# A build-time plan that holds a product back a little behind the silu step it reads: other orders on all engines of one core

## Chip, cores and metric

The kernel runs on 1 core of one Trainium2 chip. The metric is the device time of one execution in microseconds. Before the change it took 378.16 us, the median of 3 runs (378.05 to 378.83).

## What is computed

Causal attention with a forget gate, whose result goes straight into a SwiGLU block. The reference, cut to what matters:

```python
# q, k, v: (8, 8, 576, 64), f: (8, 8, 576)
cum = cumsum(log(clip(f, 1e-4, 1.0)), axis=-1)
scores = q @ k^T / sqrt(64) + cum[:, :, :, None] - cum[:, :, None, :]
attn = softmax(where(causal, -1e9, scores))
x = (attn @ v).transpose(0, 2, 1, 3).reshape(4608, 512)
g = x @ w_gate                                # 512 x 1536
out = (g * sigmoid(g) * (x @ w_val)) @ w_out  # 1536 x 512, float32
```

The inputs and the output are float32; the kernel's matrix products read bf16 and gather in float32.

## The kernel before

**Who sets the order.** The kernel is written as a list of steps, each made by `op` (L304) with the engine or engines that may run it and a cost in us for each (`act`, `dve`, `mm`, `pool`, around L313). A step names the steps that it reads (`after`), the buffers that it takes and those that it uses, and a `key`. When the kernel is built, `Plan.run` (L77) plays all steps through in a model of time: whenever an engine is free, it takes the ready step with the lowest key whose buffers can be had, and issues its instructions. The order of the instructions on each engine, and which PSUM bank or SBUF buffer a step gets, come out of this play. On the chip nothing of the modelled times is left; each engine runs its instructions in the order that it was given, and semaphores hold a reader until its data is there. A long table, `ORDER`, replaces the keys of single steps by their number; the change leaves it alone.

**When a reader becomes ready.** In the model a step ends at `busy[e]`, the time at which its engine is free for the next one. Its results are there `PIPE` later (0.2 for PE, 0.17 ACT, 0.12 DVE, 0.11 POOL), and readers on another engine, or on one of several, become ready only then. A reader whose single engine is the one that has just run the step becomes ready at `busy[e]` itself, that is, in time for the very next place on that engine. These two cases are the two pushes of the event "done":

```python
push(busy[e], "done", (o, e, True))
push(o.done, "done", (o, e, False))
```

**The work.** PE does all matrix products, ACT the exponentials and tanh, DVE (VectorE) the products of the SwiGLU, POOL (GpSimd) masks and some copies and sums, SP most of the DMAs.

- *Attention*, head by head: `score` (PE, L703) in four groups of 320 to 512 columns, `expo` (ACT, L737), `mask` of the diagonal blocks (POOL, L746), `weigh` (PE, L760), which sums the values by the weights into a bank of which there is one ("o"), `invert` and `scale` (DVE, L767 and L772), which read that bank and free it, and then a transpose into `xT`: on PE by `flip` (L777), or by a DMA on SP, `cross` (L790). The heads' queries and keys come over DMAs: `narrow` (POOL's queue, L590), `turned` (SP, L599), and `rows`, the rows of decay (SP, L602).
- *The SwiGLU*, in nine token tiles of 512 tokens and twelve column blocks each. `unit` makes one block: a gate product (four matmuls of 512 columns, PE, L918), `tanh` of half the gate (ACT, L922), the `silu` step on DVE (L932), th = (th + 1) * gate, a value product (PE, L918 again), and `times` (DVE, L935), hh = th * 0.5 * value. From block 6 of tile 6 on ACT does the whole silu (L925) and DVE has no silu step. Banks for gate and value products come from a pool of four ("f").
- *The output products*. Tiles 0 to 2 take w_out as it is (`project`, PE, L976, and copies on ACT). Tiles 3 to 8 (`finish`) make seven products of halves instead of eight: DVE first makes blends of the weights once (`blend`, L948) and three sums of each pair of hh (`sums`, L960); PE makes the products (L969), and the halves are put together by ACT (`mid_copy`, L985), POOL (`both` and `apart`, L992 and L1017) and DVE (`more` and `close`, L996 and L1020) and stored by SP (L1023).

Silu and `times` have the key -5, `sums` 50000 and `blend` 40000 and up; the plan so takes a sum or a blend on DVE only where no SwiGLU step is ready.

Of the kernel before, what the change touches and what calls it, by code (L numbers as in the profile page):

```python
# [34 lines left out]
class Plan:  # L35
# [9 lines left out]
    def op(self, eng, fn, after=(), behind=(), take=(), use=(), key=0.0, ready=0.0, dma=None):  # L45
        o = Op(eng, fn, list(after), behind, list(take), list(use), key, ready, dma)
        for b in o.use:
            b.left += 1
        self.ops.append(o)
        return o  # L50
# [26 lines left out]
    def run(self, idle=None):  # L77
# [9 lines left out]
        busy = {e: 0.0 for e in engines}  # L87
# [5 lines left out]
        left, t, seq = len(self.ops), 0.0, 0  # L93
        events = []

        def push(at, kind, o):
            nonlocal seq
            seq += 1
            heapq.heappush(events, (at, seq, kind, o))
# [9 lines left out]
        while left:  # L109
# [3 lines left out]
            t = events[0][0]  # L113
            while events and events[0][0] <= t + 1e-9:
                _, _, kind, o = heapq.heappop(events)
                if kind in ("queue", "dma"):
                    for r, share in shares():
                        r[0][0] -= (t - moved) * share
                        while r and r[0][0] < 1e-6:
                            over, n = r.pop(0)  # L120
# [27 lines left out]
                elif kind == "done":  # L148
                    o, e, own = o
# [6 lines left out]
            for e in engines:  # L156
                while busy[e] <= t + 1e-9:
                    k = kind_of.get(e)
                    full = k and lanes[k][taken[k] % 8] > t
                    if e == "SP" and full:  # L160
                        break
                    ready[e] = [o for o in ready[e] if o.start is None]
                    best = None
                    for o in sorted(ready[e], key=lambda o: (o.key, o.n)):
                        if o.dma is not None and full:
                            continue
                        if self._takes(o, t):
                            best = o
                            break
                    if best is None:  # L170
                        break
                    o = best
                    o.start, o.ran = t, e
                    dur = o.eng[e]
                    if e == "PE":
                        dur *= self.clock(t)
                        self._fill(idle, busy[e], t)
                    o.fn(e)
                    busy[e] = end = t + dur
                    for s in o.then:  # L180
                        s.wait -= 1
                        if not s.wait:
                            push(max(t, s.ready), "ready", s)
                    if o.dma is not None:
                        o.lane = taken[k] % 8
                        lanes[k][o.lane] = 1e9
                        taken[k] += 1
                        push(max(end + (0.53 if o.tag == "f" else 0.9), T_SW if e == "POOL" else 0.0), "queue", o)
                        push(busy[e], "wake", None)
                    else:  # L190
                        o.done = end + self.PIPE[e]
                        push(busy[e], "wake", None)
                        push(o.done, "end", o)
                        push(busy[e], "done", (o, e, True))
                        push(o.done, "done", (o, e, False))
        return max(o.done for o in self.ops)

# [24 lines left out]
def kernel(ctx, tc, q, k, v, f, w_gate, w_val, w_out, out):  # L222
# [78 lines left out]
        lambda t: 2.0 if t < TWARM else 1.0,  # L301
    )

    def op(eng, fn, *args, tag=None, packet=20.0, **kw):  # L304
        if not isinstance(eng, dict):
            eng = {eng[0]: eng[1]}
        o = plan.op(eng, lambda e: fn(e, *args), **kw)
        o.tag, o.packet = tag, packet
        return o

    E = {"ACT": nc.scalar, "DVE": nc.vector, "POOL": nc.gpsimd, "SP": nc.sync, "PE": nc.tensor}
# [1 line left out]
    def act(n):  # L313
        return 0.055 + n / 1200

    def dve(n, psum=True):
        return (n + (75 if psum else 58)) / 960

    def mm(*cols):
        return sum(c / 2400 + 0.0025 for c in cols)  # L320
# [98 lines left out]
    def gates(parts, key):  # L419


        lds = [op(("ACT" if n % 2 else "SP", 0.45), ld_f, n, key=-1e4 + n, dma=0.1, packet=100, tag="f") for n in range(4)]
        ld1 = op(("SP", 0.5), ld_f, None, key=-39, dma=LD1, packet=50, ready=LD1_AT, behind=lds[2:3], tag="f1")
        done, s, lns = [], None, []
        for i, c in enumerate(parts):
# [42 lines left out]
    def blank(e, what):  # L468
# [46 lines left out]
        else:  # L515
            if what != "rest":
                fill32(e, VB[what][:, :, :, D:].bitcast(F32), ONE2)
            if what:
# [4 lines left out]
              after=[op(("DVE", 0.07), lambda e: nc.vector.memset(warm, 1.0), key=-30)])  # L523
# [507 lines left out]
    def unit(t, fc, t0, n, hs, lo, kk, after):  # L1031
        if (t, fc) == ALONE:
            tabled.append(op(("ACT", 1.4), turn_table, after=before + exps, key=-6, tag="table"))
        needs = [o for a, b, done in x_ready.values() if a < t0 + n and b > t0 for o in done]
        wr = [w_ready["g", fc // FCG], w_ready["v", fc // FCG]]
        bg, bv, bt = Buf(*F_POOLS(t)), Buf(*F_POOLS(t)), Buf("th")
        p, r = divmod(fc, 2)
        fresh = hs[p] is None
        if fresh:
            hs[p] = Buf("hh")  # L1040
            hs[p].first = None
        g = op(("PE", mm(*[n] * KD)), gate, wg, fc, t0, n, bg, after=needs + wr + after, behind=[] if fresh else [hs[p].gate], take=[bg] + ([hs[p]] if fresh else []), key=kk, tag=("gp", t, fc))
        if fresh:
            hs[p].gate = g
        alone = (t, fc) >= ALONE
        if alone:
            b = op(("ACT", act(n)), whole, n, bg, bt, after=[g] + tabled, take=[bt], use=[bg], key=-5, tag=("tanh", t, fc))
        else:
            b = op(("ACT", act(n)), tanh, n, bg, bt, after=[g], take=[bt], use=[bg], key=-5, tag=("tanh", t, fc))
            before.append(b)  # L1050
            b = op(("DVE", dve(n)), silu, n, bg, bt, after=[b], use=[bg, bt], key=-5, tag=("silu", t, fc))
        a = op(("PE", mm(*[n] * KD)), gate, wv, fc, t0, n, bv, after=[g], take=[bv], key=kk + 1, tag=("vp", t, fc))
        m = op(("DVE", dve(n)), times, n, bv, bt, hs[p], r, lo, 1.0 if alone else 0.5, after=[a, b, hs[p].first],
               use=[bv, bt, hs[p]], key=-5, tag=("mul", t, fc))
        if fresh:
            hs[p].first = m
        read.append((t0, t0 + n, [g, a]))
        return g, m
# [3 lines left out]
    def ffn(t, t0, n):  # L1062
        key, hs, ms = 1e5 * (t + 1), [None] * (KF // 2), []
        for fc in range(KF):
            parts = [(0, HALF), (HALF, n - HALF)] if t == 0 and fc < WIDE else [(0, n)]
            ms.append([])
            for u, (lo, w) in enumerate(parts):
                lg, m = unit(t, fc, t0 + lo, w, hs, lo, key + 100 * fc + 50 * u, [last_gate[0]])
                ms[fc].append(m)
        last_gate[0] = lg  # L1070
        tails.append((t, t0, key, hs, ms))
# [3 lines left out]
    def simple(t, t0, key, hs, ms):  # L1075
        for q in range(2):
            bo = Buf("ot")
            for h in range(2):
                bf, a = Buf("f"), None
                for g in range(0, KF // 2, 2):  # L1080
                    a = op(("PE", mm(*[DM] * 4)), project, hs, q, h, bf, (g, g + 1),
                           after=[x for m in ms[2 * g : 2 * g + 4] for x in m] + [w_ready["o", c] for c in range(NCO)] + [a],
                           take=[] if g else [bf], use=[hs[g], hs[g + 1]] + ([bf] if g else []), key=key + 2000 + 200 * q + 100 * h + g, tag=("fo", t, q, h))
                plain.append(a)
                c = op(("ACT", act(DM)), out_copy, h, bf, bo, after=[a] + (o_out2 + regrouped if t == 0 else []), take=[] if h else [bo],
                       use=[bf] + ([bo] if h else []), key=-4, tag=("ot", t, q, h))
                op(("SP", 0.7), store, t0 + h * HALF + q * P, h, bo, after=[c], use=[bo], key=-4, dma=1.0, packet=90, tag=("out", t, q, h))
# [95 lines left out]
    for t, t0 in enumerate(range(0, N_TOK, MT)):  # L1183
        ffn(t, t0, MT)
    for r in tails[:QUICK]:
        simple(*r)
    ready = [w_ready["o", c] for c in range(NCO)]
    blended = [op({e: f((KF // 2) * HALF // 2) + 0.35 * (n // 2 == 1) for e, f in BLEND_ON.items()}, blend, n, after=ready, key=BLEND_KEY + n, ready=BLEND_AT, tag=("blend", n)) for n in range(6)]
    blended += [op({e: f((KF // 2) * HALF // 2) for e, f in BLEND_ON.items()}, blend, n, after=blended[:6] + plain, key=BLEND_KEY + n, ready=BLEND_AT, tag=("blend", n)) for n in range(6, 10)]
    for r in tails[QUICK:]:  # L1190
        finish(*r, blended)
# [17 lines left out]


QUICK = 3


def F_POOLS(t):
    return ("f",) + tuple((x, WIDE_AT, 1e9) for x in "sot")
# [152 lines left out]
```

## Time and profile before

| | before |
|---|---|
| median of 3 runs | 378.16 us |
| the profiled execution | 378.08 us |
| its span, from the first to the last instruction | 376.4 us |
| granted TensorE clock, mean | 1.00 |
| busy DVE, of the span | 249.4 us, 66% |
| `times` (L935): count, mean of one | 112, 667 ns |
| `silu` on DVE (L932): count, mean of one | 82, 656 ns |
| `sums` (L960): count, mean of one | 108, 384 ns |

The profile is one execution. A row in order of time gives the start from the span's begin and the length, both in us, then engine, line, operation, what is written and read, shapes, and how many of the same stand together; in brackets the time for which the engine waited ahead of it and what ended that wait. A line of stretches gives from:to and length, and then for PE, the weight loads of PE, DVE, ACT and POOL the busy time and the number of instructions, after that the granted clock, the mean share of the DMA engines, and GB/s. The chain of waits is the work that ended last, followed back from the end, each step to what released it. Ends of matmuls are modelled, and so is the busy time of PE.

### The profile page before, as it was taken

To read this page: it belongs to the slowest core of one execution; us is meant where nothing else is said; L and a number is where in the kernel's file an instruction comes from. 1 tells how busy PE (TensorE), PEld (TensorE's weight loads), DVE (VectorE), ACT (ScalarE), POOL (GpSimd) and SP (SyncE) were. 2 spreads that over 40 slices of the span, in tenths; PEclk is the share of its full clock that TensorE was granted. 3 is DMA by queue.
4 is the path that set the end of the run, shared out by engine and by line. 5 is a ranking of instruction groups with operands and counts; after the bars stand their busy time and mean duration, and the time that the engine had idled before them with its cause. 6 is when DMAs were issued, how large, how long until landed. Compare 5 with 4: busy or idle time off the path is not lost.

```text
span 376.4 us, 9092 instructions
## 1 busy us (share of the span) xinstructions
PE 368.8 (98%) x3427; PEld 233.6 (62%) x3427; DVE 249.4 (66%) x575; ACT 214.4 (57%) x438; POOL 161.4 (43%) x388
## 2 busy tenths in 40 slices
PE   8999999999999999999999999999999999999996
PEld 5667655455565555555685558655887776467465
DVE  7979886277526674499737994598638844753664
ACT  7999962265656754746576467555774433333332
POOL 8897546033633643465376437732462013003000
PEclk9999999999999999999999999999999999999999
DMA  8999998859988998999699999995325003002003
GB/s 145 192 198 195 206 204 151 185 100 180 174 187 169 166 189 160 228 191 180 117 160 200 228 149 143 243 206 99 72 74 93 2 2 111 2 0 81 33 0 114
DMA packets 125163, 52.01 MB, mean 138 GB/s; under 512 B 111823, under 2 KB 119695, under 8 KB 124351
## 3 DMA queue, kind: packets, MB, share of 16 engines
q1 hardware_dynamic: 108478, 35.95, 49.2%
q0 software_dynamic: 16288, 15.14, 26.9%
q8 instruction: 27, 0.44, 0.5%
q10 hardware_dynamic: 352, 0.34, 0.3%
q14 instruction: 18, 0.14, 0.1%
HBM read 38.56 MB, written 17.07 MB: 148 GB/s over the span
## 4 chain that ended last, share of the span: by engine, by line
PE 94%; DMA 2%; DVE 1%; POOL 1%; ACT 1%; issue 1%; DVEq 0%; POOLq 0%
PE ps L918 49%; PE ps L969 14%; PE ps L703 10%; PE ps L976 8%; PE ps L760 8%; DMA su<-in_k_dram 2%; PE ps L721 1%; PE ps L777 1%; PE ps L578 1%; POOL su L554 1%; PE ps L729 0%; PE ps L1201 0%; ACT PT L737 0%; DVE hh L935 0%; DVE xn L772 0%
## 5 line engine op out<-in xcount | busy, mean ns | idle before, releaser
L918 PE MATMUL ps<-xT,wv 128*128 128x512 bf16 (+2 forms) x496 | 111.7, 351 | 0.0
L918 PE MATMUL ps<-xT,wg 128*128 128x512 bf16 (+2 forms) x496 | 111.5, 351 | 0.0
L737 ACT ACTIVATE PT<-ps 128x384 bf16<-128x384 f32 (+2 forms) x192 | 91.6, 510 | 14.8 <-PE ps L703 9.7
L935 DVE SCALAR_TENSOR_TENSOR hh<-th,ps 128x512 bf16<-128x512 f32 (+1 forms) x112 | 74.5, 667 | 21.1 <-PE ps L918 12.9
L922 ACT ACTIVATE th<-ps 128x512 f32<-128x512 f32 (+1 forms) x82 | 47.2, 577 | 54.1 <-PE ps L918 51.8
L746 POOL TENSOR_SCALAR_AFFINE_SELECT PT<-PT 128x128 bf16<-128x128 bf16 (+1 forms) x192 | 54.1, 288 | 44.1 <-ACT PT L737 38.5
L918 PEld LDWEIGHTS <-wg 128*128 128x128 bf16 x496 | 45.1, 97 | 37.9
L918 PEld LDWEIGHTS <-wv 128*128 128x128 bf16 x496 | 45.0, 97 | 38.1
L932 DVE SCALAR_TENSOR_TENSOR th<-th,ps 128x512 f32<-128x512 f32 (+1 forms) x82 | 53.7, 656 | 19.7 <-ACT th L922 19.6
L703 PE MATMUL ps<-QK 68*128 68x256 bf16 x392 | 63.9, 261 | 0.4 <-ACT PTa L737 0.4
L746 POOL TENSOR_SCALAR_AFFINE_SELECT PTa<-PTa 128x256 bf16<-128x256 bf16 x64 | 26.3, 413 | 80.3 <-ACT PTa L737 79.5
L760 PE MATMUL ps<-VB,PT 128*128 128x65 bf16 x768 | 42.0, 193 | 0.0
L703 PEld LDWEIGHTS <-QK 68*128 68x128 bf16 x392 | 31.5, 97 | 14.0 <-issue 0.6
L760 PEld LDWEIGHTS <-PT 128*128 128x128 bf16 x768 | 34.2, 97 | 9.3 <-POOL PT L746 0.9
L737 ACT ACTIVATE PTa<-ps 128x384 bf16<-128x384 f32 x64 | 30.9, 488 | 15.4 <-PE ps L703 14.8
L767 DVE RECIPROCAL rc<-ps 128x5 f32<-128x5 f32 (+2 forms) x68 | 12.8, 188 | 39.6 <-PE ps L760 39.3
L969 PEld LDWEIGHTS <-su 128*128 128x128 bf16 x360 | 34.8, 97 | 4.6
L960 DVE TENSOR_TENSOR su<-hh 128x512 bf16<-128x512 bf16 (+1 forms) x108 | 36.7, 384 | 0.9
L925 ACT ACTIVATE th<-ps 128x512 f32<-128x512 f32 x30 | 17.9, 596 | 32.1 <-PE ps L918 32.1
L976 PE MATMUL ps<-wo,hh 128*128 128x512 bf16 x144 | 34.8, 379 | 0.0
L772 DVE TENSOR_TENSOR xn<-ps,rc 128x320 bf16<-128x320 f32 (+2 forms) x72 | 32.4, 454 | 2.2
L969 PE MATMUL ps<-wt,su 128*128 128x256 bf16 x216 | 29.0, 272 | 0.0
(97 smaller groups left out, 323.1 us busy)
## 6 DMA issues: line engine op xcount, KB each, us to landing
out_dram<-ot SPq DMA_DIRECT2D x32, 256.0 KB
natv<-in_v_dram SPq DMA_DIRECT2D x25, 256.0 KB
qk_d<-in_q_dram POOLq DMA_DIRECT2D x24, 144.0 KB, 3.6
qk_d<-in_k_dram POOLq DMA_DIRECT2D x24, 144.0 KB, 4.3
wv<-in_moe_w_val_dram POOLq DMA_DIRECT2D x3, 512.0 KB, 10.6
wg<-in_moe_w_gate_dram POOLq DMA_DIRECT2D x3, 512.0 KB, 12.4
wo<-in_moe_w_out_dram POOLq DMA_DIRECT2D x4, 384.0 KB, 14.1
VB<-in_v_dram POOLq DMA_DIRECT2D x7, 128.0 KB, 8.9
```

What stands on the lines that cost most here:

```text
L703: nc.tensor.matmul(s[:, c : c + w], QK[:KR, hqk[p].i, 1, j * S + kt * P : j * S + (kt + 1) * P], QK[:KR, hqk[p].i, 0, j * S + q0 : j * S + ...
L737: nc.scalar.activation(place(h, i)[:, OFFS[i] : OFFS[i] + c], ps(bs)[:, :c], AF.Exp, scale=0.125)
L746: nc.gpsimd.affine_select(out=d, in_=d, pattern=pat, compare_op=ALU.is_ge, fill=0.0, base=0, channel_multiplier=-1,)
L760: nc.tensor.matmul(o[:, lo : lo + D + 1], pt[:, c : c + P], VB[hvb[b].i][:, kt, hb, : D + 1], start=first and n == 0, stop=last and n == l ...
L772: nc.vector.tensor_mul(XN[bx.i][:, qb : qb + nq, j], o, r)
L918: nc.tensor.matmul(ps(bf)[:, a:b], w[:, ko, fc * P : (fc + 1) * P], xT[:, ko, at : at + b - a], start=ko == 0 and a == 0, stop=ko == KD - ...
L922: nc.scalar.activation(TH[bt.i][:, :n], ps(bf)[:, :n], AF.Tanh, scale=0.5)
L932: nc.vector.scalar_tensor_tensor(out=t, in0=t, scalar=1.0, in1=ps(bf)[:, :n], op0=ALU.add, op1=ALU.mult)
L935: nc.vector.scalar_tensor_tensor(out=HH[bh.i][:, r, lo : lo + n], in0=TH[bt.i][:, :n], scalar=by, in1=ps(bf)[:, :n], op0=ALU.mult, op1=ALU ...
L960: E[e].tensor_tensor(out=o, in0=x, in1=y, op=f)
L969: nc.tensor.matmul(ps(bf)[:, c * HALF : (c + 1) * HALF], left(g)[:, q * P : (q + 1) * P], right[:, g], start=opens and g == 0, stop=g == K ...
L976: nc.tensor.matmul(ps(bf), HH[hs[g].i][:, r, lo : lo + P], wo[:, 2 * g + r], start=g + r == 0, stop=2 * g + r == KF - 1)
```

## The change

The event that tells a reader on the same engine that its data is there is pushed `o.raw` later. Only one kind of step has a `raw` that isn't 0: `silu` on DVE, with the new constant RAW = 0.17. Its one reader on the same engine is the `times` of the same block. In the model the engine still is free at `busy[e]`, so a step that is ready then is taken, and `times` is ready 0.17 us later. Nothing else changes in the list of steps; the orders and buffers that the plan deals out are made anew. Lines after 1211 stand one lower.

```diff
-                        push(busy[e], "done", (o, e, True))
+                        push(busy[e] + o.raw, "done", (o, e, True))
                         push(o.done, "done", (o, e, False))
...
-    def op(eng, fn, *args, tag=None, packet=20.0, **kw):
+    def op(eng, fn, *args, tag=None, packet=20.0, raw=0.0, **kw):
...
-        o.tag, o.packet = tag, packet
+        o.tag, o.packet, o.raw = tag, packet, raw
...
-            b = op(("DVE", dve(n)), silu, n, bg, bt, after=[b], use=[bg, bt], key=-5, tag=("silu", t, fc))
+            b = op(("DVE", dve(n)), silu, n, bg, bt, after=[b], use=[bg, bt], key=-5, raw=RAW, tag=("silu", t, fc))
...
 QUICK = 3
+RAW = 0.17
```

## The prediction

> **What bounds the kernel now.** I read the page first: its list of engines, then the chain that ended last. After it the busy time of each engine by stage, and last the order in time around each place where PE stops.
>
> ```profile
> span 376.4 us, 9092 instructions
> ...
> PE 368.8 (98%) x3427; PEld 233.6 (62%) x3427; DVE 249.4 (66%) x575; ACT 214.4 (57%) x438; POOL 161.4 (43%) x388
> ...
> PE 94%; DMA 2%; DVE 1%; POOL 1%; ACT 1%; issue 1%; DVEq 0%; POOLq 0%
> ```
>
> PE is busy for 98% of the span and holds 94% of the chain. No other engine is near. So the time falls only where PE stands still, or rises where it is made to. The stages show where that is:
>
> ```profile
> 157.00:177.50 20.50, 20.50 (x162) 11.13 (x161) 19.56 (x40) 12.65 (x27) 11.25 (x25) 1.00 1.12 200
> 177.50:183.50 6.00, 4.93 (x42) 2.56 (x41) 5.68 (x14) 2.33 (x6) 1.73 (x5) 1.00 0.55 101
> 183.50:198.40 14.90, 14.90 (x194) 13.12 (x194) 6.39 (x17) 10.98 (x24) 10.48 (x27) 1.00 0.93 164
> ...
> 286.00:363.50 77.50, 77.50 (x531) 47.73 (x527) 46.92 (x100) 26.44 (x44) 7.96 (x8) 1.00 0.10 34
> ```
>
> After the times of a stretch come PE, PEld, DVE, ACT and POOL. PE loses 1.07 us of the six from 177.5 on (6.00 less 4.93), and nothing in the stages beside them. But a busy PE is a modelled one, so I go by starts. In the stage before, DVE works 19.56 of 20.50 us: there alone it has no room. From 286 on PE never stops, and the order of the end does not change, so what is won or lost before 286 reaches the end whole.
>
> **What the change does to the orders.** It removes and adds no instruction: the work on each engine is the same. It moves them. In the changed kernel's order, which its build gives without times, PE's groups stand as before up to 53 us, and later too but for six places, one of which is the whole stretch from 183 to 199. ACT differs only in that stretch, POOL and SP in two places each. DVE changes most: of 82 silu steps 69 were followed at once by their own product, and 39 are now. The other 30 have something between, nearly always one instruction: a sum of `sums`, a blend, a reciprocal or another silu.
>
> **What one such separation is worth.** These are DVE's instructions in order of time, then PE's and one of ACT's; the column after the start is the recorded length.
>
> ```profile
> 172.86 0.42 DVE L960 TENSOR_TENSOR su<-hh 128x512 bf16<-128x512 bf16 x1
> 173.19 0.68 DVE L932 SCALAR_TENSOR_TENSOR th<-th,ps 128x512 f32<-128x512 f32 x1
> 173.98 0.69 DVE L935 SCALAR_TENSOR_TENSOR hh<-th,ps 128x512 bf16<-128x512 f32 x1
> 174.58 1.25 DVE L960 TENSOR_TENSOR su<-hh 128x512 bf16<-128x512 bf16 x3
> 175.76 0.68 DVE L932 SCALAR_TENSOR_TENSOR th<-th,ps 128x512 f32<-128x512 f32 x1
> 176.36 0.47 DVE L960 TENSOR_TENSOR su<-hh 128x512 bf16<-128x512 bf16 x1
> 176.75 0.68 DVE L935 SCALAR_TENSOR_TENSOR hh<-th,ps 128x512 bf16<-128x512 f32 x1
> 177.34 0.18 DVE L767 RECIPROCAL rc<-ps 128x5 f32<-128x5 f32 x1
> 177.56 0.49 DVE L772 TENSOR_TENSOR xn<-ps,rc 128x320 bf16<-128x320 f32 x1
> ```
>
> ```profile
> 175.26 0.25 PE L760 MATMUL ps<-VB,PT 128*128 128x65 bf16 x3
> 175.35 0.33 PE L703 MATMUL ps<-QK 68*128 68x64 bf16 x2
> 175.52 1.03 PE L918 MATMUL ps<-xT,wg 128*128 128x512 bf16 x4
> 176.38 0.30 PE L703 MATMUL ps<-QK 68*128 68x320 bf16 x1
> 176.52 1.03 PE L918 MATMUL ps<-xT,wv 128*128 128x512 bf16 x4
> 178.10 0.25 PE L760 MATMUL ps<-VB,PTa 128*128 128x65 bf16 x3 [0.56 <-DVE xn L772]
> ```
>
> ```profile
> 173.70 0.60 ACT L922 ACTIVATE th<-ps 128x512 f32<-128x512 f32 x1 [0.31 <-PE ps L918]
> ```
>
> The product that reads the silu just before it starts 0.79 us after it (173.19 to 173.98), 0.11 after its end. An instruction that reads something else starts 0.60 after (175.76 to 176.36, 173.98 to 174.58). With a sum between, silu to product takes 0.99, and that holds a sum's 0.39; apart they cost 0.79 and 0.33 (172.86 to 173.19). A separation so saves 0.13 us behind a sum, up to 0.19 behind another.
>
> The Trainium skill speaks against this: "VectorE: DVE Perf Modes", section "The DRAIN you can't avoid", says that the next Vector op waits until the pipe is empty, and that no chaining avoids it, though it adds that an op that is not held starts earlier. By its first half a separation would be worth 0, which is the first rival below. The rows go with the second half: 0.60 comes before the silu's recorded end, and only the reader waits past it.
>
> **The stall at 177.4.** Four 512-column matmuls take PE 0.86 us (175.52 to 176.38). So the weighted sum of the next head could start at 177.38, and started at 178.10: 0.72 lost. It waited for the scaling at 177.56, which empties the only bank for these sums. That had nothing left to wait for but DVE itself: its matmuls had run by 175.35. In the stage from 157 on there are nine silu steps, and eight stand ahead of their own product:
>
> ```profile
> 157.00:177.50 20.50, 6.11 (x9) 1.00 1.12 200
> ```
>
> ```profile
> 166.21 5.18 PE ps L918 x24
> ```
>
> All eight are separated. They put DVE ahead by 8 x 0.13 to 8 x 0.19, that is 1.0 to 1.5 us, before the silu at 175.76. The stall needs 0.72. The product at 176.75 could start 0.72 sooner, at 176.03, since its value matmuls stand on PE ahead of the row at 175.26; the silu could start at 175.04, since its tanh ended at 174.30. So I take all of it: **-0.72 us**.
>
> What is held back meanwhile: each product is now behind a sum (0.34) or a blend (up to 0.64), and it frees the bank of the next value products. The cover is in the last row above, the chain's: six groups of PE without a gap from 166.21 on. Stepping DVE's rows forward with the pitches above, the tightest of these groups finds its bank free 0.86 us before its turn. If that cover were gone, one blend would cost PE at most 0.64 - 0.19 = 0.45.
>
> **Three waits that PE's order drops.** Each pair of rows is the work before a wait and the group that waited.
>
> ```profile
> 53.06 0.33 PE L703 MATMUL ps<-QK 68*128 68x64 bf16 x2
> 53.35 0.45 PE L777 MATMUL ps<-ident,xn 128*128 128x128 bf16 x5
> ...
> 98.86 1.03 PE L976 MATMUL ps<-wo,hh 128*128 128x512 bf16 x4
> 99.84 0.25 PE L760 MATMUL ps<-VB,PTa 128*128 128x65 bf16 x3
> ...
> 208.62 1.03 PE L918 MATMUL ps<-xT,wv 128*128 128x512 bf16 x4
> 209.77 0.25 PE L760 MATMUL ps<-VB,PTa 128*128 128x65 bf16 x3
> ```
>
> Two such score matmuls take 0.17 (175.35 to 175.52): 53.06 + 0.17 leaves 0.12 lost. 98.86 + 0.86 leaves 0.12, and 208.62 + 0.86 leaves 0.29. In the new order a score and a whole value product stand before the first of the late groups, two score matmuls (0.17) before the second, and a gate product (0.86) before the third. Each is longer than its wait: **-0.53 us**. The displaced work was ready.
>
> **What stays, and one wait that is new.** The next head begins at 182:
>
> ```profile
> 182.00 0.55 PE L703 MATMUL ps<-QK 68*128 68x256 bf16 x4
> ...
> 182.37 0.49 ACT L737 ACTIVATE PTa<-ps 128x384 bf16<-128x384 f32 x1 [0.43 <-PE ps L703]
> ...
> 182.91 0.33 PE L703 MATMUL ps<-QK 68*128 68x64 bf16 x2 [0.36 <-ACT PTa L737]
> ...
> 182.94 0.40 POOL L746 TENSOR_SCALAR_AFFINE_SELECT PTa<-PTa 128x256 bf16<-128x256 bf16 x1 [4.12 <-ACT PTa L737]
> ...
> 183.39 0.26 PE L760 MATMUL ps<-VB,PTa 128*128 128x65 bf16 x3 [0.15 <-POOL PTa L746]
> ...
> 183.42 0.29 POOL L746 TENSOR_SCALAR_AFFINE_SELECT PT<-PT 128x128 bf16<-128x128 bf16 x1
> ...
> 183.63 0.82 PE L969 MATMUL ps<-wo,hh 128*128 128x256 bf16 x6
> ```
>
> Scores, exponential and mask follow each other here with nothing of PE's between. The two pauses are 0.36 and 0.15 by the last column. By starts they are more: four matmuls of at most 256 columns take half of 0.86, so 0.91 - 0.43 = 0.48 is lost ahead of 182.91, and 0.48 - 0.17 = 0.31 ahead of 183.39, 0.79 in all. They move along with PE and stay: 0. Right behind, the old order has the first output product at 183.63. The new one has five weighted sums that read the mask of 183.42. It ends at 183.71, and PE follows a mask by 0.05 (183.34 to 183.39): 183.76, **+0.13 us**. From there to 198 the output products and heads of attention are dealt out anew, in the same number of product groups. I stepped through them with the pitches above: each bank and mask comes free before it is needed, the tightest by about 0.05. I take 0. If it fails, a head costs up to the 0.79.
>
> **Queues.** SP issues a pair's decay rows, which a score reads at 188.5, only behind a crossing that waits for DVE:
>
> ```profile
> 182.52 0.63 SPq L602 DMA_DIRECT2D QK<-dec_d  x1
> ...
> 188.50 0.55 PE L703 MATMUL ps<-QK 68*128 68x256 bf16 x4
> ```
>
> In the new order they stand ahead of it, while that score comes some two us sooner: it has at least the 6 us of before, so 0. ACT's copies and POOL's adds move by one to three places among exponentials and masks; the stage's 10.98 and 10.48 busy of 14.90 cover them. If the cover were gone, the 0.79 of a head is the price again.
>
> **Sum.** -0.72 - 0.53 + 0.13 = -1.12. The profiled execution took 378.08 us (376.4 of it the span, the rest around it unchanged), 0.08 under the median of 378.16. 378.08 - 1.12 = **377.0 us**.
>
> **The other ways.**
> - **A separation saves nothing.** DVE takes the same time whatever follows, so the stall at 177.4 stays and only the dropped waits count: -0.53 + 0.13, 377.7; with a blend's 0.45 exposed, 378.1. For it speaks that the chain holds 1% of DVE, so that a faster DVE may meet nothing; against it the starts above, and that this one stall hangs on DVE.
> - **The dealt-out stage stalls.** Between 183.5 and 198.4 weighted sums come as little as one product group (0.66) behind their scores, and the way through ACT and POOL took 1.02 (182.37 to 183.39). Each head that waits in full gives back 0.79: from two heads on (378.6) the kernel is slower than before, with three 379.4. For it speaks the new wait at the stage's very start; against it that most heads keep a product group and other scores between.
> - **More is won.** The pauses at 182 close too, because ACT and POOL are free earlier: 377.0 - 0.79 = 376.2. Against it: they hang on PE's own scores.
>
> **Chances.** 0.60 for the forecast (376.5 to 377.4), 0.20 for the first rival, 0.16 for the second (379.4 its time; 0.03 of the 0.16 for only one or two heads), 0.04 for the third. About 0.2% (0.76 us) is what a measurement can tell from no change. So faster means under 377.4: the forecast and the third rival less 0.01 that its range spills, 0.63. No change is the first rival, the spill, and the second with one or two heads: 0.24. Slower is the rest of the second, 0.13. The range of 8 in 10 goes from 376.4 to 378.8: it leaves out the third rival and most of the three heads.
>
> **What will show it.** Right: no gap of PE ahead of the weighted sums near 177, a reciprocal there about 0.7 us or more ahead of the products around it, product starts 0.60 after a silu with a sum between them; and one short gap, under 0.2, just ahead of the first output product near 183. Wrong: PE's busy time per stretch falling from 183 to 198, or waits for ACT or POOL of 0.3 and more at the weighted sums of that stage; or a DVE that still works without a break up to a late scaling.

## Result and profile after

The changed kernel took 376.73 us, the median of 6 runs (376.44 to 377.18), beside 378.14 us for the kernel before (378.04 to 378.83, 6 runs): 1.41 us less, a ratio of 0.9961 with a 95% interval of 0.9948 to 0.9974. The forecast was 377.0, faster by 1.1. The profiled execution of the changed kernel is the slowest of its six, 377.18 us with a span of 375.5.

The list of engines and the first line of the chain of waits, of the changed kernel:

```profile
span 375.5 us, 9089 instructions
...
PE 369.6 (98%) x3427; PEld 234.2 (62%) x3427; DVE 246.3 (66%) x575; ACT 214.2 (57%) x438; POOL 161.8 (43%) x388
...
PE 93%; DMA 2%; POOL 2%; issue 0%; DVE 0%; ACT 0%; DVEq 0%; POOLq 0%
```

DVE has the same 575 instructions and 3.1 us less of busy time; the share of DVE in the chain has gone from 1% to 0%. The stages around the stall, in the changed kernel (columns as before: from:to, length, PE, PEld, DVE, ACT, POOL, clock, DMA share, GB/s):

```profile
157.00:177.50 20.50, 20.50 (x164) 11.19 (x162) 20.26 (x43) 12.65 (x27) 11.18 (x26) 1.00 1.12 202
177.50:183.50 6.00, 5.49 (x49) 2.84 (x48) 5.90 (x14) 2.98 (x7) 1.97 (x6) 1.00 0.79 148
183.50:198.40 14.90, 14.90 (x202) 13.23 (x200) 5.62 (x16) 11.53 (x25) 11.71 (x30) 1.00 0.86 160
```

In the stage from 157 on DVE gets 43 instructions done where it got 40. PE now loses 0.51 of the six us from 177.5 on (6.00 less 5.49) where it lost 1.07, and does 49 matmuls there instead of 42.

Busy shares say that something was won, not where. The starts of the same matmul in both traces do. Both traces have all 3427, so the n-th of the one is compared with the n-th of the other, at places where the order of PE is the same in both:

| n-th matmul | before | after | after less before |
|---|---|---|---|
| 600 | 38.25 | 38.79 | +0.54 |
| 780 | 59.11 | 59.51 | +0.40 |
| 1200 | 110.17 | 110.46 | +0.29 |
| 1740 | 176.52 | 176.81 | +0.29 |
| 1744, the weighted sums that stalled | 178.10 | 177.67 | -0.43 |
| 2040 | 207.02 | 206.66 | -0.36 |
| 2100 | 215.62 | 214.97 | -0.65 |
| 2220 | 228.86 | 228.00 | -0.86 |
| 3360 | 365.18 | 364.31 | -0.87 |

The profiled execution starts 0.54 late, in the first 20 us, which differ from run to run. From there it gains 0.14, 0.11, 0.72, gives back 0.07, and gains 0.29 and 0.22: 1.41 in all, the same as the difference of the medians. Such a column, the lateness of one trace against another, is what the experiments below are read by; "by starts" means it. Five of the traces below lack some 35 of the 3427 records; there the matmuls of the two traces are matched group by group.

DVE and then PE around the old stall, in order of time in the changed kernel:

```profile
174.62 0.69 DVE L932 SCALAR_TENSOR_TENSOR th<-th,ps 128x512 f32<-128x512 f32 x1
175.23 0.42 DVE L960 TENSOR_TENSOR su<-hh 128x512 bf16<-128x512 bf16 x1
175.57 0.68 DVE L935 SCALAR_TENSOR_TENSOR hh<-th,ps 128x512 bf16<-128x512 f32 x1
176.16 0.19 DVE L767 RECIPROCAL rc<-ps 128x5 f32<-128x5 f32 x1
176.38 0.49 DVE L772 TENSOR_TENSOR xn<-ps,rc 128x320 bf16<-128x320 f32 x1
```

```profile
176.81 1.03 PE L918 MATMUL ps<-xT,wv 128*128 128x512 bf16 x4
177.67 0.25 PE L760 MATMUL ps<-VB,PTa 128*128 128x65 bf16 x3
...
183.07 0.30 PE L703 MATMUL ps<-QK 68*128 68x320 bf16 x1
183.34 0.32 PE L760 MATMUL ps<-VB,PT 128*128 128x65 bf16 x5
```

The scaling that frees the bank stood at 177.56 and stands at 176.38, in a trace that is 0.29 late there: DVE is 1.47 ahead of its old self. From the stage's first silu to this scaling DVE does the same 39 instructions in both kernels, in 20.46 us before and 19.00 after. The weighted sums at 177.67 follow the value product's 0.86 with no gap. The new wait is at 183.34: one score matmul of 0.13 starts at 183.07, so 0.14 is lost.

### The profile page after: what moved, and what is told of

The parts are those of the page before. It is cut to its first block, busy times and chain, and to the rows that moved or that the text cites. A ratio compares the mean times of both kernels' runs of the same rounds, so it can differ in the third digit from the quotient of the medians.

```text
span 375.5 us, 9089 instructions
## 1 busy us (share of the span) xinstructions
PE 369.6 (98%) x3427; PEld 234.2 (62%) x3427; DVE 246.3 (66%) x575; ACT 214.2 (57%) x438; POOL 161.8 (43%) x388
## 4 chain that ended last, share of the span: by engine, by line
PE 93%; DMA 2%; POOL 2%; issue 0%; DVE 0%; ACT 0%; DVEq 0%; POOLq 0%
PE ps L918 50%; PE ps L969 14%; PE ps L703 10%; PE ps L976 8%; PE ps L760 8%; DMA VB<-in_v_dram 2%; PE ps L578 1%; PE ps L777 1%; POOL PTa L746 1%; POOL su L554 1%; PE ps L721 1%; PE ps L729 0%; POOL xT L554 0%; POOL VB L608 0%; DVE ot L1013 0%
## 5 line engine op out<-in xcount | busy, mean ns | idle before, releaser
L746 POOL TENSOR_SCALAR_AFFINE_SELECT PT<-PT 128x128 bf16<-128x128 bf16 (+1 forms) x192 | 55.0, 293 | 42.6 <-ACT PT L737 36.9
L703 PE MATMUL ps<-QK 68*128 68x256 bf16 x392 | 63.0, 261 | 0.4 <-ACT PTa L737 0.4
L960 DVE TENSOR_TENSOR su<-hh 128x512 bf16<-128x512 bf16 (+1 forms) x108 | 38.0, 386 | 0.9
```

What stands on the lines that cost most here:

```text
L703: nc.tensor.matmul(s[:, c : c + w], QK[:KR, hqk[p].i, 1, j * S + kt * P : j * S + (kt + 1) * P], QK[:KR, hqk[p].i, 0, j * S + q0 : j * S + ...
L746: nc.gpsimd.affine_select(out=d, in_=d, pattern=pat, compare_op=ALU.is_ge, fill=0.0, base=0, channel_multiplier=-1,)
L960: E[e].tensor_tensor(out=o, in0=x, in1=y, op=f)
```

## Experiments

All but the two that change no order by hand work in one way. The plan's play is run as it is, but each step is written into a list instead of being issued; single steps are moved in the list, and then the list is issued. Banks and buffers stay as the plan dealt them. So one engine's order can be changed while the others keep theirs.

```diff
-                    o.fn(e)
+                    self.log.append((o, e))
...
+def ahead(log, tag, of):     # issue the step `tag` just ahead of the step `of`
+    x = log.pop(find(log, tag))
+    log.insert(find(log, of), x)
...
+    edit(log)
+    for o, e in log:
+        (o.fn if isinstance(o, Op) else o)(e)
```

Tags: ("mul", t, b) is `times` of block b of tile t, "gp" and "vp" are the gate and value products, ("s", h, i) and ("o", h, i) a score and a weighted sum of head h, "rcp" and "scale" the head's `invert` and `scale`. `behind` puts a step just behind another. Times are medians, each beside runs of the kernel before on the same chip; ratios are against those.

### Separation alone, on DVE alone

```diff
+APART = {0: ("blend", 4), 1: ("blend", 6), 2: ("blend", 8), 3: ("sum", 3, 0, 0),
+         4: ("sum", 3, 0, 1), 5: ("sum", 3, 0, 2), 6: ("sum", 3, 1, 0), 7: ("sum", 3, 1, 1)}
+    for fc, tag in APART.items():
+        ahead(log, tag, ("mul", 3, fc))
```

> The orders of before on PE, ACT, POOL and SP; on DVE alone, in tile 3, eight silu steps (blocks 0 to 7) get one blend or sum between them and their product, an instruction that stood a little later. My theory: each separation gives DVE 0.13 to 0.19 us, 1.0 to 1.5 together, so the PE wait of 0.72 us ahead of the weighted sums at 178.1 goes, and nothing else does: 378.14 - 0.72 = 377.4. Rival (a separation saves nothing, and the changed kernel won that wait through the plan's other orders): 378.1, with the wait still 0.7.

Measured: 377.91 beside 378.37, ratio 0.9983 (0.9975 to 0.9992). PE at the old stall, and at the place where a part of the gain went, with DVE's rows for the latter:

```profile
177.08 1.03 PE L918 MATMUL ps<-xT,wv 128*128 128x512 bf16 x4
177.94 0.25 PE L760 MATMUL ps<-VB,PTa 128*128 128x65 bf16 x3
```

```profile
159.25 0.47 PE L703 MATMUL ps<-QK 68*128 68x64 bf16 x3
159.82 0.25 PE L760 MATMUL ps<-VB,PTa 128*128 128x65 bf16 x3
```

```profile
157.99 0.55 DVE L948 TENSOR_TENSOR wt<-wo 128x768 bf16<-128x768 bf16 x1
158.46 0.68 DVE L935 SCALAR_TENSOR_TENSOR hh<-th,ps 128x512 bf16<-128x512 f32 x1
159.06 0.18 DVE L767 RECIPROCAL rc<-ps 128x5 f32<-128x5 f32 x1
159.28 0.49 DVE L772 TENSOR_TENSOR xn<-ps,rc 128x320 bf16<-128x320 f32 x1
```

The stall is gone with PE's order untouched: 177.08 + 0.86 = 177.94. But a new wait of 0.28 stands at 159.82 (three score matmuls take 0.30 from 159.25): the blend now stands ahead of the product, and so ahead of the scaling at 159.28 that the weighted sums wait for. By starts the kernel wins 0.43 in all. The theory holds for the stall; "nothing else does" was wrong.

The same eight separations, and the value product that the changed kernel has at this place:

```diff
+    ahead(log, ("vp", 3, 1), ("o", 34, 0))
```

> As the run with eight separations, and one PE move of the changed kernel: the value product of block 1 of tile 3 ahead of the weighted sums near 159. My theory: the wait of 0.28 that the eight left at 159.8 was the scaling held back by a blend; the value product covers it, so the trace wins the whole 0.72 between 150 and 180. Rival (the wait at 159.8 has another cause): it stays 0.2 to 0.3 and the gain 0.45.

Measured: 377.38 beside 378.32, ratio 0.9978 (0.9967 to 0.9988); by starts 0.70 less in all, and 0.72 of it won between 176 and 178.

```profile
158.94 0.47 PE L703 MATMUL ps<-QK 68*128 68x64 bf16 x3
159.25 1.03 PE L918 MATMUL ps<-xT,wv 128*128 128x512 bf16 x4
160.11 0.25 PE L760 MATMUL ps<-VB,PTa 128*128 128x65 bf16 x3
```

The value product is the cover: 159.25 + 0.86 = 160.11, no wait. So the 0.72 is DVE's time, and the plan's new PE order near 159 is what keeps the blend from taking 0.28 of it back.

### Three separations instead of eight

```diff
+APART = {5: ("sum", 3, 0, 1), 6: ("sum", 3, 1, 0), 7: ("sum", 3, 1, 1)}
```

> As the run with eight separations, but only three (tile 3, blocks 5, 6 and 7). My theory: 3 x 0.13 to 3 x 0.19 = 0.39 to 0.57 us off a wait of 0.72, so 0.15 to 0.33 of it stays in the trace, and the time is 377.6 to 377.8. Rival (only the order counts, not DVE's time): the wait is 0.7 or 0.

```profile
177.70 1.03 PE L918 MATMUL ps<-xT,wv 128*128 128x512 bf16 x4
178.88 0.25 PE L760 MATMUL ps<-VB,PTa 128*128 128x65 bf16 x3 [0.15 <-DVE xn L772]
```

177.70 + 0.86 leaves 0.32 of the 0.72: three separations took off 0.40, inside the expected range, and the rival falls. That is not 0.13 each, though all three have a sum between. Two of the three sums, in order of time, each with its silu and its product, and what POOL did beside the second:

```profile
170.71 0.68 DVE L932 SCALAR_TENSOR_TENSOR th<-th,ps 128x512 f32<-128x512 f32 x1
171.31 0.42 DVE L960 TENSOR_TENSOR su<-hh 128x512 bf16<-128x512 bf16 x1
171.64 0.68 DVE L935 SCALAR_TENSOR_TENSOR hh<-th,ps 128x512 bf16<-128x512 f32 x1
...
173.97 0.68 DVE L932 SCALAR_TENSOR_TENSOR th<-th,ps 128x512 f32<-128x512 f32 x1
174.57 0.70 DVE L960 TENSOR_TENSOR su<-hh 128x512 bf16<-128x512 bf16 x1
175.19 0.68 DVE L935 SCALAR_TENSOR_TENSOR hh<-th,ps 128x512 bf16<-128x512 f32 x1
```

```profile
174.38 0.61 POOL L329 CAST VB<-natv 128x512 bf16<-128x512 f32 x1
```

Each silu is left after 0.60 instead of 0.79, which is 0.19 won, three times 0.56. The first sum then takes 0.33, as sums do elsewhere; the second, beside a cast of POOL, takes 0.62. The eight sums of the stage take 2.96 us in all, from start to start, where they took 2.77 before. So 0.56 less 0.19 leaves about 0.4.

The time hardly shows it: 378.31 beside 378.37, ratio 0.9993 (0.9984 to 1.0002), where 377.6 to 377.8 was expected. By starts the profiled execution, the slowest of its twelve, lost 0.37 at another place, where a score waited for its rows of decay.

```profile
152.25 0.54 PE L703 MATMUL ps<-QK 68*128 68x256 bf16 x4 [0.20 <-DMA QK<-dec_d]
```

Nothing is edited ahead of that place, and the kernel before has no such wait in its trace; it is in two other profiled executions below. Whether the median has that wait too isn't shown. What three separations are worth is so read from the stall, not from the time.

### The separations taken out of the changed kernel

```diff
+    for fc, tag in {0: ("blend", 4), 1: ("blend", 6), 2: ("blend", 8), 3: ("sum", 3, 0, 0),
+                    5: ("sum", 3, 0, 1), 6: ("sum", 3, 1, 0), 7: ("sum", 3, 1, 1)}.items():
+        behind(log, tag, ("mul", 3, fc))
+    behind(log, ("scale", 35), ("rcp", 35))
+    behind(log, ("silu", 3, 4), ("scale", 35))
```

> The changed kernel, but in tile 3, blocks 0 to 7, each product follows its silu at once again on DVE; all other engines keep the changed orders. My theory: DVE is late again by what the separations gave, so PE waits 0.5 to 0.8 us ahead of the weighted sums near 177.7, and the time is 376.73 + 0.5 to 0.8 = 377.2 to 377.5. Rival (the other orders removed the wait): 376.7.

Measured: 378.00 beside 378.37, ratio 0.9985 (0.9975 to 0.9995), where the changed kernel has 0.9961: about 0.9 us lost again, by starts 1.0, more than the 0.5 to 0.8 expected.

```profile
177.30 1.03 PE L918 MATMUL ps<-xT,wv 128*128 128x512 bf16 x4
178.67 0.25 PE L760 MATMUL ps<-VB,PTa 128*128 128x65 bf16 x3 [0.34 <-POOL PT L746]
```

```profile
178.12 0.49 DVE L772 TENSOR_TENSOR xn<-ps,rc 128x320 bf16<-128x320 f32 x1
```

177.30 + 0.86 leaves 0.51 at the old place. The row names a mask of POOL, but the weighted sums start 0.55 after the scaling's start, as they did in the kernel before (177.56 to 178.10); the two came within 0.1 of each other. Another 0.25 is lost at 169, where a gate product now waits, and the last 0.25 in the stage from 183 to 199, which the changed kernel's other orders had dealt out for an earlier DVE. The rival, no loss, falls.

### Separations everywhere else

```diff
+    for o, m, x in zip(dve, dve[1:], dve[2:]):
+        if o.tag and o.tag[0] == "silu" and m.tag == ("mul",) + o.tag[1:] and not (o.tag[1] == 3 and o.tag[2] < 9):
...
+            l = log.pop(next(i for i, (p, e) in enumerate(log) if p is x))
+            log.insert(next(i for i, (p, e) in enumerate(log) if p is m), l)
```

The lines left out pass over an instruction that, by the plan's times, wasn't ready when the product began.

> The orders of before on PE, ACT, POOL and SP; on DVE alone, every silu outside tile 3's blocks 0 to 8 that was followed at once by its product gets the DVE instruction behind that product between them, where it was ready by then. My theory: outside the stage from 157 to 177.5 DVE has idle time, so its gain is worth nothing there: the same five PE waits as before, and a time like before's, at most 0.2 less if the mask behind the wait of 0.14 at 222.2 meets fewer of DVE's sums. Rival (DVE's time counts everywhere): 0.4 less than before or more, with the waits at 53.4, 99.8 and 209.8 shorter.

Measured: 378.37 beside 378.32, ratio 0.9998 (0.9988 to 1.0008). In the trace 54 of the 82 silu steps are followed at once by a product, where 70 were. By starts the waits at 53, 100, 178 and 210 are all there, within 0.03 of before. One wait of 0.07 at 184.8 has become 0.23, and the 0.14 at 222 is gone: masks that met other sums of DVE and took 0.50 instead of 0.34 and 0.29 instead of 0.57, to which the last experiment comes back.

```profile
51.45 0.69 DVE L932 SCALAR_TENSOR_TENSOR th<-th,ps 128x512 f32<-128x512 f32 x1 [0.54 <-ACT th L922]
```

Ahead of the wait at 53 DVE came earlier than before and lost it again in this idle time, in which it waits for a tanh. So DVE's time is worth nothing where DVE idles afterwards. For the waits at 100 and 210 the run shows less: ahead of 100 no silu was separated after DVE's last idle time, and ahead of 210 one was (207.07), but from it to the reciprocal DVE takes 2.34 where it took 2.35, as the sums there took longer. An earlier DVE at these two waits was not made.

### PE's moves alone

```diff
+    ahead(log, ("s", 14, 3), ("flip", 4))
+    ahead(log, ("vp", 0, 9), ("flip", 4))
+    ahead(log, ("s", 21, 1), ("o", 20, 0))
+    ahead(log, ("gp", 4, 5), ("o", 45, 0))
```

> The orders of before on DVE, ACT, POOL and SP; on PE alone the three moves of the changed kernel: a score and a value product ahead of the flip at 53.4, two score matmuls ahead of the weighted sums at 99.8, a gate product ahead of those at 209.8. My theory: the three waits of 0.12, 0.12 and 0.29 go, the one of 0.72 at 178.1 stays: 378.14 - 0.53 = 377.6. Rival (the waits go with DVE's earlier end, and the moved work is late elsewhere): 378.1.

Measured: 378.34 beside 378.37, ratio 1.0000 (0.9988 to 1.0011).

```profile
55.83 0.81 PE L918 MATMUL ps<-xT,wg 128*128 128x512 bf16 x3
56.72 0.25 PE L760 MATMUL ps<-VB,PTa 128*128 128x65 bf16 x3
```

```profile
56.17 0.49 DVE L772 TENSOR_TENSOR xn<-ps,rc 128x320 bf16<-128x320 f32 x1
```

The three waits are gone in this trace, but by starts 0.25 is lost at 56.7, where the next head's weighted sums wait for a scaling 0.55 before them. (The record of one of the four gate matmuls is missing.) Two later losses, 0.40 at 151.7 on rows of decay and 0.16 at 169, hide the rest in the profiled execution. So the first of the moves was no win by itself. I had left out a step that the changed kernel has there:

```diff
+    ahead(log, ("s", 15, 2), ("o", 11, 0))
+    ahead(log, ("s", 15, 3), ("o", 11, 0))
```

> As the run with three PE moves, and a fourth that the changed kernel also has: the last two scores of the head behind the flip at 53.4 stand ahead of the next weighted sums. My theory: the wait of 0.24 that the three moves left at 56.7 goes, and the three waits of 0.12, 0.12 and 0.29 stay away, 0.5 less than before in the trace between 45 and 225, the wait of 0.72 at 178.1 still there. Rival (what one PE move gives, a later wait takes back): no less than before.

Measured: 378.03 beside 378.32, ratio 0.9990 (0.9979 to 1.0001); by starts 0.54 less, 0.15 at 53, 0.12 at 100 and 0.27 at 210, and nothing given back. The interval of the ratio still reaches 1, so it is the trace that shows the gain. The stall of 0.72 at 178 stands.

### Does the value of RAW matter

The changed kernel itself, and beside it one with a smaller constant:

```diff
-RAW = 0.17
+RAW = 0.01
```

> The changed kernel itself, beside the two that follow: 1.4 less than before, 376.7 to 377.0.

> The changed kernel with RAW = 0.01 in place of 0.17: 37 silu steps still get something between them and their product, the stretch from 183 to 199 is dealt out as in the changed kernel, and so is the value product near 159, but the three PE moves at 53, 100 and 210 us are gone. My theory: the separation comes from holding the product back at all, so the 0.72 at 178 stays won, and the three waits of 0.12 to 0.29 are back: 0.5 more than the changed kernel, 377.2 to 377.4, 0.9 less than before. Rival (the value 0.17 itself carries the gain): like before, within 0.3.

Measured beside 378.62: the changed kernel 377.09, ratio 0.9962 (0.9951 to 0.9974); with 0.01 377.56, ratio 0.9975 (0.9967 to 0.9983). The time came out as expected beside its neighbours, 0.5 above the changed kernel and 1.1 below the kernel before (377.56 itself is above the expected 377.2 to 377.4), but not by the way expected: the waits at 53 and 100 are back with 0.25 together, the one at 210 isn't.

```profile
209.55 1.03 PE L918 MATMUL ps<-xT,wv 128*128 128x512 bf16 x4
210.42 0.25 PE L760 MATMUL ps<-VB,PTa 128*128 128x65 bf16 x3
```

With no gate product between, the weighted sums still start without a wait (209.55 + 0.86 = 210.41), since DVE is earlier beside PE here: the scaling they wait for moved by 0.59 (209.23 to 209.82), PE's value product by 0.93 (208.62 to 209.55). In the changed kernel DVE has about the same lead, so that wait is won twice over there. The lead is there already at the last silu ahead of it (206.66 to 207.19); the sum that now stands behind this silu adds nothing, with 2.41 from the silu to the reciprocal where it was 2.35. What in the newly dealt-out stage before it gives the lead isn't shown. In the profiled execution, the slowest of its twelve, a score near 152 waits 0.64 for its rows of decay, and another 0.13 is lost at 141; whether the median has these waits isn't shown, so the other half of the 0.5 is open.

### Closing the pauses at 182, and a version that beats both

On the changed kernel:

```diff
+    ahead(log, ("s", 38, 0), ("vp", 3, 11))
+    ahead(log, ("s", 38, 1), ("vp", 3, 11))
+    behind(log, ("o", 47, 3), ("s", 48, 1))
+    behind(log, ("o", 57, 2), ("fo", 5, 0, 3, 0))
```

> The changed kernel with four PE moves of its own: the first two score groups of the head at 181.6 go ahead of the value product before them, and two weighted sums that waited 0.18 at 224.0 and 0.09 at 266.5 go behind work that was ready. My theory: the value product takes the place of the pauses of 0.53 and 0.32, with 0.3 left ahead of the first weighted sums, since the tanh of the last block stands ahead of the exponential on ACT; the product of the last block waits for DVE anyway. 0.5 + 0.2 to 0.3 less than the changed kernel: 376.0. Rival (the value product's delay is met at the output products): 376.5 to 376.7.

Measured: 376.81 beside 378.32, ratio 0.9952 (0.9934 to 0.9970). One of the eight executions took 2169.77 us, and no trace shows why; the other seven lie between 375.75 and 378.07, with a median of 376.68. The time is so nearer to the rival's 376.5 to 376.7 than to the expected 376.0, and it can't be told from the changed kernel's (0.9948 to 0.9974). By starts from 47 us on it wins 1.99 where the changed kernel wins 1.41, so 0.58 more; its profiled execution was 2 us late in its first 35. It misses the expected 0.7 to 0.8 since the wait of 0.14 behind the pauses became one of 0.19, at 184.3, and one of 0.16 opened at 186.76, 0.54 after the scaling that those weighted sums wait for:

```profile
185.94 0.82 PE L969 MATMUL ps<-wo,hh 128*128 128x256 bf16 x6
186.76 0.25 PE L760 MATMUL ps<-VB,PTa 128*128 128x65 bf16 x3
```

```profile
186.22 0.49 DVE L772 TENSOR_TENSOR xn<-ps,rc 128x320 bf16<-128x320 f32 x1
```

A group of six output matmuls takes 0.66 from start to start, so 185.94 + 0.66 leaves 0.16. The same moves were therefore made on the orders of before instead, whose stage from 183 on has no weighted sums at that place, together with all that the runs above had shown to win: the eight separations, the value product near 159, and the moves at 53, 100 and 210.

```diff
...
+    ahead(log, ("s", 38, 0), ("vp", 3, 11))
+    ahead(log, ("s", 38, 1), ("vp", 3, 11))
+    behind(log, ("o", 46, 3), ("s", 47, 2))
+    ahead(log, ("s", 48, 0), ("o", 47, 3))
+    ahead(log, ("s", 48, 1), ("o", 47, 3))
+    behind(log, ("o", 57, 2), ("fo", 5, 0, 3, 0))
```

> The orders of before, with the eight separations of tile 3 on DVE and, on PE, the value product near 159, the moves at 53, 100 and 210 us, the scores of 182 ahead of the value product before them, and the three late weighted sums near 222, 225 and 267 behind work that was ready. My theory: the waits of before go one by one, 0.72 + 0.54 + 0.55 + 0.14 + 0.16 + 0.09 = 2.2 less than before, 376.0, 0.7 less than the changed kernel. Rival (a win moves to the next wait): 376.6 or more.

Measured: 376.47 beside 378.62, ratio 0.9945 (0.9932 to 0.9958): 2.15 less than before, where 2.2 was expected, and 0.6 less than the 377.09 of the changed kernel on the same chip. All five executions (376.19 to 376.60) are below all five of the changed kernel there (376.66 to 377.50). By starts 2.1.

```profile
180.73 0.55 PE L703 MATMUL ps<-QK 68*128 68x256 bf16 x4
181.12 1.03 PE L918 MATMUL ps<-xT,wv 128*128 128x512 bf16 x4
181.98 0.33 PE L703 MATMUL ps<-QK 68*128 68x64 bf16 x2
182.44 0.27 PE L760 MATMUL ps<-VB,PTa 128*128 128x65 bf16 x3
182.54 0.30 PE L703 MATMUL ps<-QK 68*128 68x320 bf16 x1
182.68 0.82 PE L969 MATMUL ps<-wo,hh 128*128 128x256 bf16 x6
```

The value product fills the time in which the exponential and the mask run; one wait of 0.29 is left (181.98 + 0.17 to 182.44), and the output products follow at once. It has the lowest median and the lowest ratio of this study.

### One move for a mask

Back to the 0.14 at 222, on which the prediction had nothing:

```diff
+    for n in (2, 1, 0):
+        behind(log, ("sum", 4, 4, n), ("scale", 46))
```

> The orders of before, with one edit on DVE: the three sums that stand at 221.2, beside the mask that took 0.57 us, go behind the scaling at 223.8. My theory: a POOL mask is slowed by DVE's sums, which read two tensors of SBUF; without them the mask takes 0.29 and the PE wait of 0.14 at 222.2 goes, while masks that now meet the sums near 224.5 become longer. Rival (the mask is long for another reason, or the wait hangs on ACT): mask and wait stay as they were.

POOL and DVE around it, in the kernel before and then in this one:

```profile
221.55 0.57 POOL L746 TENSOR_SCALAR_AFFINE_SELECT PT<-PT 128x128 bf16<-128x128 bf16 x1 [1.09 <-ACT PT L737]
...
222.96 0.62 POOL L746 TENSOR_SCALAR_AFFINE_SELECT PT<-PT 128x128 bf16<-128x128 bf16 x2 [0.43 <-ACT PT L737]
```

```profile
221.21 1.05 DVE L960 TENSOR_TENSOR su<-hh 128x512 bf16<-128x512 bf16 x3
```

```profile
221.54 0.29 POOL L746 TENSOR_SCALAR_AFFINE_SELECT PT<-PT 128x128 bf16<-128x128 bf16 x1 [1.09 <-ACT PT L737]
...
222.95 0.80 POOL L746 TENSOR_SCALAR_AFFINE_SELECT PT<-PT 128x128 bf16<-128x128 bf16 x2 [0.62 <-ACT PT L737]
```

```profile
221.09 0.69 DVE L932 SCALAR_TENSOR_TENSOR th<-th,ps 128x512 f32<-128x512 f32 x1
```

The same mask takes 0.57 beside the sums and 0.29 beside a silu, and the wait of PE behind it is gone: by starts 0.14 less there. (A single execution of each took 377.89 and 378.16, which is less apart than executions of one kernel.) Of the two masks that a row shows from 222.95 on, the second now meets the sums and takes 0.42 where it took 0.24. The masks near 224.5, which were expected to become longer, didn't: the sums are over by then.

## Why the prediction was right

**The stall at 177.4, -0.72: right, in place, size and cause.** By starts 0.72 was won there, and eight separations on DVE alone win it with PE's order held (once the blend is covered), three win 0.40 of it, and taking them out of the changed kernel opens 0.51 of it again. DVE came 1.47 ahead, the upper end of the 1.0 to 1.5. "There alone it has no room" was not right: DVE works 5.68 of 6.00 us in the next stage too, but none of PE's other waits there hung on it.

**What one separation is worth, 0.13 to 0.19: the upper end was right, for a sum too.** A silu is left after 0.60 instead of 0.79, and a sum behind it takes 0.33 as elsewhere; eight times 0.19 is the 1.47. The 0.13 rested on a single sum, of 0.39, which had a mask of POOL beside it (176.26 to 176.54). Such a meeting lengthens a sum wherever it stands; it is no part of a separation's price. As the stall needed 0.72 of the 1.0 to 1.5, the forecast did not depend on it. The rival that a separation saves nothing falls. The half of the Trainium skill's rule on which it stood ("VectorE: DVE Perf Modes", section "The DRAIN you can't avoid": the next op waits for the empty pipe) does not describe these rows; the other half, that an op which isn't held starts earlier, agrees with them: 174.62 to 175.23, 0.61 after a silu that ends 0.69 after its start.

**What is held back meanwhile: right in its sum, wrong about its cover.** The prediction looked at six product groups from 166 on and found banks free early enough. What a blend held back was a scaling at 159, not a bank, and the cover was a value product that the plan had moved there, one of the six places of PE that the text counted but did not price. Without it 0.28 is lost, inside the bound of 0.45.

**The dropped waits, -0.53: right in size** (0.54 by starts in the run with PE's moves alone). "Each is longer than its wait" and "the displaced work was ready" was too quick for the first: a single move there won 0.15 and lost 0.25 three us later, and only the following pair of scores, moved as well, kept it. And the wait at 210 has two winners, the gate product and a DVE that comes to it earlier.

**The new wait, +0.13: right**, 0.14 at 183.34. **The dealt-out stage, 0: right, and so are the queues, 0:** no score of the stage waits for its rows of decay. The wait of 0.07 at 184.8 went, so that from 178 to 207 0.07 is given back where 0.13 was forecast. No head stalled for ACT or POOL, so the second rival falls; that the stage has little room was right too, as a DVE that is late again loses about 0.25 in it. **The pauses at 182** moved along, 0.53 and 0.32 in both traces; the third rival, that they close because ACT and POOL are free earlier, falls. They can be closed in part, by moving work of PE into them.

**The sum, -1.12, was short by 0.3.** What is missing is the 0.22 from 215 on, and 0.07 at 184.8. Of the larger, 0.14 at 222 is a step that the sum doesn't have: it took POOL's masks to be of one length wherever they fall, and moving DVE's sums changes how long a mask beside them takes. The other 0.08 was not traced to a cause.

## What to carry to other kernels

A build-time planner that lets a reader follow its producer at once on the same engine pays the engine's own latency each time, here 0.19 us. Letting a ready instruction in between saves it, but that is worth time only where a wait of the busiest engine hangs on this one, and this one does not idle before it. When one order is changed alone, look for what the moved instruction now holds back: both single edits here that seemed plain wins, the eight separations and the first PE move, lost part or all of their gain at a place within a few us of the edit, and a second move there kept it. For differences under 0.3% compare the starts of the same matmul in two traces: the runs of one and the same kernel lay 0.4 to 2.3 us apart here, the one of 2169.77 us left out.

## What the runs showed of the hardware

**A mask on POOL is slowed by DVE's sums.** In the trace of before 114 of 128 masks of 128x128 meet no sum or blend of DVE (L960, L948), and take 282 to 305 ns. Seven lie beside one for over 80% of their length, and take 341 to 620 ns, 488 in the mean. Which of the two began first decides: in eight of the 14 masks that meet a sum or blend it had begun before the mask, and these take 341 to 620 ns; in five it began 0.10 us or more after the mask, and in one it was all but over, and these take 284 to 292. The move of three sums shows that this is cause and not chance, at 221.5; the mask takes 0.29 as well in the changed kernel and in the run with separations everywhere else, where the sums are over by then or begin later. The sums suffer too: beside POOL's work they took up to 0.62 from start to start (174.57 in the run with three separations), while 53 of them without it took 0.33 to 0.34 in the trace of before. The Trainium skill has the rule, "GPSIMD Engine Reference", section "8. Key points": GpSimd shares its interfaces to SBUF with VectorE, and contends with Vector instructions that have two inputs in SBUF. A sum has two such inputs; a silu has one, the other lies in PSUM. Here it costs up to 0.33 us for one mask.

**Rows of decay come late in some executions.** A score near 152 waited for them in three of the profiled executions (0.37, 0.40 and 0.64 by starts) and not in the others, with nothing edited ahead of it in one of the three. Why the rows come later in those executions stays open.
